# Main products of two MLPs: moving columns and outputs in eights, 32 words apart

## The chip, the cores and the metric

One NeuronCore of a Trainium2 chip runs the kernel. The metric is the device time of one execution in microseconds (us); a number for a kernel is the median of several executions. The profile is of one execution, taken by the hardware profiler, in which time is counted from the first to the last instruction (the span).

## What is computed

12480 tokens of 128 numbers go through an attention over 32 inducing points, applied twice, then through two MLPs of width 2048. The first has a leaky activation with a slope per hidden unit, the second the square of a ReLU. All is float32.

```python
def mab(q, kv):                       # attention of q over kv
    a = softmax(scale * (q @ kv.T))
    return a @ kv
h = mab(inducing, x)                  # 32 x 128
x = mab(x, h)                         # 12480 x 128
h = x @ w_in                          # first MLP, 128 -> 2048 -> 128
x = (np.maximum(h, 0.0) + alpha * np.minimum(h, 0.0)) @ w_out
h = np.maximum(x @ w2_in, 0.0)        # second MLP, 128 -> 2048 -> 128
out = h * h @ w2_out
```

## The kernel before

A first stage (to about 45 us) loads and transposes x, sums up the first attention and converts weights. Then a main loop runs over 25 tiles of tokens, 21 of 512 tokens, 3 of 448 and one of 384 (`WIDTHS`, line 19), and over 16 chunks of the hidden width in each. Tokens lie along the moving columns of TensorE's products, so a product is 512, 448 or 384 columns wide.

The order is written out by hand: a loop over steps s (lines 816 to 830) issues, for each s, `l1_a` (chunk s of the first MLP's first layer), `l2_a` and `l2_split` (the second MLP's first layer, 24 and 25 steps behind), `l2_b` and `l1_b` (the second layers, 28 and 3 steps behind), and whatever `plan` holds for that step (attention of the next four tiles, conversion of weights). The engines take their instructions in that order.

Products are made in float32r. To keep accuracy an operand is split into a high and a low part, and `three` (line 688) adds up high x high, low x high and high x low in one PSUM bank. So a step has ten products: one in `l1_a` (line 679; there the tile `a_s` holds the high and low parts in its partitions), three each in `l1_b`, `l2_a` and `l2_b` (lines 689 to 691). One more per tile, `end_y1` at line 707, adds the linear part of the leaky activation. Each product has its own 128x128 weights, so each comes with a weight load (PEld in the profile).

In a step ScalarE makes g1h (line 683), r (723) and g2h (732) and VectorE makes g1l (685) and sq (725); GpSimd makes g2l (734), except in the last 24 steps, when VectorE does. They read PSUM or SBUF contiguously and write the tiles that the next products stream.

In the memory layout of this program all weights of main products and all 512-wide moving tiles start at word 8 of their group of 32 words. Tiles narrower than 512 live in 512-wide buffers, and `columns` (line 118) gives them the place from word 40 of the buffer on, that is word 16 of a group of 32. A 512-wide tile fills its buffer.

Of the kernel before, what the change touches and what calls it, by code (L numbers as in the profile page):

```python
# [19 lines left out]
T = 512  # L20
# [10 lines left out]
def attention_then_two_mlps(ctx: ExitStack, tc, x, inducing, w_in, w_out, alpha, w2_in, w2_out, out):  # L31
# [3 lines left out]
    nc = tc.nc  # L35
# [3 lines left out]
    P = 128  # L39
# [29 lines left out]
    def free_bank():  # L69
        turn[0] += 1  # L70
        return ms_bank() if turn[0] % 2 or main_loop else y2_bank()
# [3 lines left out]
    def keep_tile(name, shape, dt=F32):  # L75
        return keep.tile(shape, dt, name=name, tag=name)
# [39 lines left out]
    xT = keep_tile("xT", [P, N])  # L116

    def columns(v, w):
        return v if w == T else v[:, 40 : 40 + w]

    w1s = keep_tile("w1s", [P, DFF], F32R)
    wo_hi = keep_tile("wo_hi", [P, NCH, P], F32R)
# [8 lines left out]
    v_s = keep_tile("v_s", [P, P], F32R)  # L131
# [163 lines left out]
    def scores(g):  # L295
        b = ms_bank()
        for i, (t0, n, _, _) in enumerate(groups1[g]):
            nc.tensor.matmul(
                b[i * M : (i + 1) * M, :n], indT, xT[:, t0 : t0 + n], start=True, stop=True,
                tile_position=(0, i * M),  # L300
            )
        return b[:, :n]
# [64 lines left out]
    b = free_bank()  # L367
# [4 lines left out]
    for g in range(last):  # L372
        if g:
            run(convs[g - 1][:2])
        b = scores(g)
# [18 lines left out]
        if g == 2:  # L394
            b = y2_bank()
# [6 lines left out]
    b = scores(last)  # L402
# [6 lines left out]
    b = y2_bank()  # L409
# [9 lines left out]
    b = ms_bank()  # L419
# [25 lines left out]
    b = y1_bank()  # L445
# [15 lines left out]
    def new_a_s(t):  # L461
        a_s[t] = columns(att.tile([P, T], F32R, name="a_s", tag="a_s", bufs=5), wide[t])
        return a_s[t]
# [211 lines left out]
    def l1_a(i, other_bank):  # L675
        t, c = divmod(i, NCH)
        b = h2_bank() if other_bank else h1_bank()
        a, w = a_s[t], wide[t]
        nc.tensor.matmul(b[:, :w], w1s[: a.shape[0], c * P : (c + 1) * P], a, start=True, stop=True)  # L679

        tag = "g2" if i < EARLY and i % 2 else "g1"
        hi = columns(wk.tile([P, T], F32R, name="g1h", tag=tag + "h", bufs=4), w)
        nc.scalar.activation(hi, b[:, :w], AF.Relu)  # L683
        lo = columns(wk.tile([P, T], F32R, name="g1l", tag=tag + "l", bufs=4), w)
        nc.vector.scalar_tensor_tensor(lo, b[:, :w], 0.0, f32(hi), op0=ALU.max, op1=ALU.subtract)  # L685
        g1[i] = hi, lo

    def three(b, w_hi, w_lo, hi, lo, start, stop):
        nc.tensor.matmul(b, w_hi, hi, start=start, stop=False)  # L689
        nc.tensor.matmul(b, w_lo, hi, start=False, stop=False)  # L690
        nc.tensor.matmul(b, w_hi, lo, start=False, stop=stop)  # L691

    def l1_b(i):
        t, c = divmod(i, NCH)
        if c == 0:
            y1_cur[t] = y1_bank() if t != 1 else y2_bank()
        b = y1_cur[t][:, : wide[t]]
        hi, lo = g1.pop(i)
        three(b, wo_hi[:, c, :], wo_lo[:, c, :], hi, lo, c == 0, False)
        if c == NCH - 1 and t:  # L700
            end_y1(t)

    def end_y1(t):
        w = wide[t]
        b = y1_cur.pop(t)[:, :w]
        a = a_s.pop(t)
        nc.tensor.matmul(b, v_s[: a.shape[0]], a, start=False, stop=True)  # L707
        hi = columns(wk.tile([P, T], F32R, name="y1h", tag="y1h", bufs=2), w)
        nc.scalar.copy(hi, b)
        lo = columns(wk.tile([P, T], F32R, name="y1l", tag="y1l", bufs=2), w)  # L710
        nc.vector.tensor_tensor(lo, b, f32(hi), op=ALU.subtract)
        y1_split[t] = hi, lo

    def l2_a(i):
        t, c = divmod(i, NCH)
        w = wide[t]
        b = h2_bank()[:, :w]
        cols = slice(c * P, (c + 1) * P)
        three(b, *(w2[tag][:, cols] for tag in W2["w2_in"]), *y1_split[t], True, True)
        if c == NCH - 1:  # L720
            del y1_split[t]
        r = wk.tile([P, T], F32, name="r", tag="r", bufs=2)[:, :w]
        nc.scalar.activation(r, b, AF.Relu)  # L723
        sq = wk.tile([P, T], F32, name="sq", tag="sq", bufs=3)[:, :w]
        nc.vector.tensor_tensor(sq, b, r, op=ALU.mult)  # L725
        rr[i] = sq
# [10 lines left out]
    def l2_b(i):  # L737
        t, c = divmod(i, NCH)
        if c == 0:
            y2_cur[t] = y2_bank()  # L740
        w = wide[t]
        b = y2_cur[t][:, :w]
        hi, lo = g2.pop(i)
        cols = slice(c * P, (c + 1) * P)
        three(b, *(w2[tag][:, cols] for tag in W2["w2_out"]), hi, lo, c == 0, c == NCH - 1)
        if c == NCH - 1:

            o = wk.tile([P, T], F32, name="o", tag="o", bufs=2)[:, :w]
            del y2_cur[t]
            if t == NT - 1:  # L750
                return last_rows(b, o)
            nc.vector.transpose(o, b)
            dst = out[first_token[t] : first_token[t + 1], :].rearrange("(b i) (a j) -> a i b j", i=M, j=M)
            for a in range(P // M):
                nc.sync.dma_start(
                    out=dst[a], in_=o[a * M : (a + 1) * M, :].rearrange("i (b j) -> i b j", j=M)
                )
# [41 lines left out]
    at(13, convs[7][LO])  # L799
    at(16, split_v)  # L800
    at(20, end_y1, 0)
    for tiles in groups[1:]:
        for k, v in enumerate(second_attention(tiles)):
# [12 lines left out]
    for s in range(total + LAG2 + LAG2B + 4):  # L816
        if s < total:
            l1_a(s, s < LAG2 and s % 2)
        if 0 <= s - LAG2 < total:
            l2_a(s - LAG2)  # L820
        if 0 <= s - LAG2 - 1 < total:
            l2_split(s - LAG2 - 1)

        ends = [(l1_b, i) for i in l1_b_at.get(s, [])]
        if 0 <= s - LAG2 - LAG2B < total:
            ends.insert(0 if ends and ends[0][1] % NCH == 0 else len(ends), (l2_b, s - LAG2 - LAG2B))
        for f, i in ends:
            f(i)
        for f in plan.pop(s, []):
            f()  # L830
# [30 lines left out]
```

## Time and profile before

| | |
|---|---|
| median of 3 executions | 961.35 us (961.16 to 964.46) |
| span of the profiled execution | 959.4 us (the time of that execution as a whole isn't listed apart) |
| TensorE busy | 949.3 us, 99% of the span |
| weight loads (they overlap products) | 787.6 us, 82% |
| ScalarE, VectorE, GpSimd busy | 727.4, 649.9, 536.9 us |
| granted TensorE clock, mean | 0.999 of full speed |

Busy time of TensorE is made of lengths of pipelined instructions, of which several are under way at once; how fast products follow each other is read from their starts in the timeline. In a row of section 5 of the page, the numbers behind the bar are the busy time in us, the mean length of one in ns, and the idle time of the engine before them.

### The profile page before, as it was taken

What the parts mean: (1) busy time and instruction counts of PE and PEld (TensorE: products, weight loads), DVE (VectorE), ACT (ScalarE), POOL (GpSimd) and SP (SyncE); (2) the same over time, 40 slices, a digit from 0 to 9 for tenths busy, and PEclk for the clock granted to TensorE, in tenths of its full rate; (3) what the DMA queues carried; (4) which work ended last, traced back from release to release, by engine and by line L of the source; (5) the groups of instructions that cost most, each with busy time, mean ns of one, the idle gap of its engine ahead of it and who ended that gap; (6) DMA issues with size and microseconds to landing.
All of it is one profiled execution on the core that took longest, in us unless ns stands there. A gap on an engine that the chain in (4) does not pass through costs nothing.

```text
span 959.4 us, 13675 instructions
## 1 busy us (share of the span) xinstructions
PE 949.3 (99%) x4560; PEld 787.6 (82%) x4560; DVE 649.9 (68%) x1013; ACT 727.4 (76%) x1333; POOL 536.9 (56%) x435
## 2 busy tenths in 40 slices
PE   9989999999999999999999999999999999999998
PEld 7667778888878888878888878888888888899997
DVE  5788767666667766667666667766666766666677
ACT  5779777777777777777777777777777777777776
POOL 2548755655555655555665555565555665555530
PEclk9999999999999999999999999999999999999999
DMA  9542000020000020000020000020000020000000
GB/s 343 163 111 82 1 12 12 9 47 12 1 12 12 3 52 12 1 12 12 1 55 12 1 12 1 12 55 1 12 12 1 12 48 1 12 12 4 8 11 19
DMA packets 64551, 29.00 MB, mean 30 GB/s; under 512 B 52208, under 2 KB 57440, under 8 KB 64480
## 3 DMA queue, kind: packets, MB, share of 16 engines
q1 hardware_dynamic: 64000, 27.52, 11.5%
q8 instruction: 36, 0.59, 0.3%
q10 hardware_dynamic: 480, 0.61, 0.2%
q14 instruction: 35, 0.29, 0.1%
HBM read 14.80 MB, written 6.39 MB: 22 GB/s over the span
## 4 chain that ended last, share of the span: by engine, by line
PE 89%; ACT 2%; DVE 1%; issue 1%; POOL 0%; POOLq 0%; DVEq 0%
PE y L691 17%; PE y L690 17%; PE y L689 17%; PE h L689 9%; PE h L690 9%; PE h L691 9%; PE h L679 8%; PE y L707 1%; PE ms L524 1%; ACT g1h L683 0%; ACT r L723 0%; DVE mag L199 0%; ACT g2h L732 0%; ACT raw L195 0%; DVE mag L205 0%
## 5 line engine op out<-in xcount | busy, mean ns | idle before, releaser
L734 POOL TENSOR_TENSOR g2l<-sq,g2h 128x512 fp32r<-128x512 f32 (+1 forms) x376 | 480.0, 1278 | 342.6 <-ACT g2h L732 331.6
L685 DVE SCALAR_TENSOR_TENSOR g1l<-h,g1h 128x512 fp32r<-128x512 f32 (+2 forms) x400 | 270.0, 677 | 230.3 <-ACT g1h L683 225.1
L683 ACT ACTIVATE g1h<-h 128x512 fp32r<-128x512 f32 (+2 forms) x400 | 234.2, 588 | 141.9 <-PE h L679 140.7
L725 DVE TENSOR_TENSOR sq<-h,r 128x512 f32<-128x512 f32 (+2 forms) x400 | 271.1, 678 | 53.9 <-ACT r L723 16.9
L723 ACT ACTIVATE r<-h 128x512 f32<-128x512 f32 (+2 forms) x400 | 235.8, 589 | 61.2 <-PE h L691 16.8
L732 ACT CAST g2h<-sq 128x512 fp32r<-128x512 f32 (+2 forms) x400 | 240.8, 602 | 2.6 <-DVE sq L725 2.6
L679 PE MATMUL h<-a_s,w1s 128*128 128x512 f32 (+3 forms) x400 | 155.0, 389 | 2.8 <-DMA a_s<-a_lo 1.4
L689 PE MATMUL h<-y1h,w2i_hi 128*128 128x512 f32 (+2 forms) x400 | 154.3, 386 | 0.3
L690 PE MATMUL y<-g2h,w2o_lo 128*128 128x512 f32 (+2 forms) x400 | 153.8, 385 | 0.0
L691 PE MATMUL h<-y1l,w2i_hi 128*128 128x512 f32 (+2 forms) x400 | 153.8, 384 | 0.0
L690 PE MATMUL h<-y1h,w2i_lo 128*128 128x512 f32 (+2 forms) x400 | 153.7, 384 | 0.0
L691 PE MATMUL y<-g2l,w2o_hi 128*128 128x512 f32 (+2 forms) x400 | 153.7, 384 | 0.0
L689 PE MATMUL y<-g2h,w2o_hi 128*128 128x512 f32 (+2 forms) x400 | 153.7, 384 | 0.0
L691 PE MATMUL y<-g1l,wo_hi 128*128 128x512 f32 (+2 forms) x400 | 153.7, 384 | 0.0
L690 PE MATMUL y<-g1h,wo_lo 128*128 128x512 f32 (+2 forms) x400 | 153.7, 384 | 0.0
L689 PE MATMUL y<-g1h,wo_hi 128*128 128x512 f32 (+2 forms) x400 | 153.7, 384 | 0.0
L679 PEld LDWEIGHTS h<-a_s,w1s 128*128 128x128 f32 (+1 forms) x400 | 75.0, 188 | 25.3 <-DVE sq L725 4.1
L689 PEld LDWEIGHTS h<-y1h,w2i_hi 128*128 128x128 f32 x400 | 75.1, 188 | 16.1 <-DVE sq L725 1.8
L690 PEld LDWEIGHTS y<-g1h,wo_lo 128*128 128x128 f32 x400 | 75.1, 188 | 14.8
L689 PEld LDWEIGHTS y<-g1h,wo_hi 128*128 128x128 f32 x400 | 75.1, 188 | 14.3
L691 PEld LDWEIGHTS y<-g2l,w2o_hi 128*128 128x128 f32 x400 | 75.1, 188 | 14.2 <-DVE g2l L734 0.3
L691 PEld LDWEIGHTS y<-g1l,wo_hi 128*128 128x128 f32 x400 | 75.1, 188 | 13.9
(156 smaller groups left out, 664.5 us busy)
## 6 DMA issues: line engine op xcount, KB each, us to landing
out_dram<-o SPq DMA_DIRECT2D x84, 64.0 KB, 2.0
xg<-in_x_dram SPq DMA_DIRECT2D x8, 512.0 KB, 9.1
raw<-in_moe_w_in_dram SPq DMA_DIRECT2D x8, 512.0 KB, 5.7
raw<-in_moe_w_out_dram SPq DMA_DIRECT2D x8, 512.0 KB, 4.6
a_s<-a_hi SPq DMA_DIRECT2D x40, 64.0 KB, 2.0
a_s<-a_lo SPq DMA_DIRECT2D x40, 64.0 KB, 2.0
x_last<-in_x_dram SPq DMA_DIRECT2D x2, 512.0 KB, 9.9
out_dram<-o SPq DMA_DIRECT2D x12, 56.0 KB, 1.9
```

The lines of the kernel that those rows point to most:

```text
L524: nc.tensor.matmul(b[i * M : (i + 1) * M, :w], hT[:, :M], xT[:, first_token[t + 1] - w : first_token[t + 1]], start=True, stop=True, tile_ ...
L679: nc.tensor.matmul(b[:, :w], w1s[: a.shape[0], c * P : (c + 1) * P], a, start=True, stop=True)
L683: nc.scalar.activation(hi, b[:, :w], AF.Relu)
L685: nc.vector.scalar_tensor_tensor(lo, b[:, :w], 0.0, f32(hi), op0=ALU.max, op1=ALU.subtract)
L689: nc.tensor.matmul(b, w_hi, hi, start=start, stop=False)
L690: nc.tensor.matmul(b, w_lo, hi, start=False, stop=False)
L691: nc.tensor.matmul(b, w_hi, lo, start=False, stop=stop)
L707: nc.tensor.matmul(b, v_s[: a.shape[0]], a, start=False, stop=True)
L723: nc.scalar.activation(r, b, AF.Relu)
L725: nc.vector.tensor_tensor(sq, b, r, op=ALU.mult)
L732: nc.scalar.copy(hi, sq)
L734: (nc.vector if i >= total - LAG2 else nc.gpsimd).tensor_tensor(lo, sq, f32(hi), op=ALU.subtract)
```

## The change

Each main product's moving operand and output are given as a pattern of four dimensions instead of two: for a tile of w columns, column 32a + 8b + c (a from 0 to w/32 - 1, b from 0 to 3, c from 0 to 7) is taken in the order b, a, c. The moving operand and the output go through the same pattern, so every result stands where it stood. Weights, tiles, buffers and the order of instructions are as before. `columns` now gives narrow tiles the buffer from word 0 on.

```diff
     def columns(v, w):
-        return v if w == T else v[:, 40 : 40 + w]
+        return v[:, :w]
+
+    def eights(v):
+        return v.rearrange("p (a b c) -> p b a c", b=4, c=8)
...
-        nc.tensor.matmul(b[:, :w], w1s[: a.shape[0], c * P : (c + 1) * P], a, start=True, stop=True)
+        nc.tensor.matmul(
+            eights(b[:, :w]), w1s[: a.shape[0], c * P : (c + 1) * P], eights(a), start=True, stop=True
+        )
...
     def three(b, w_hi, w_lo, hi, lo, start, stop):
+        b, hi, lo = eights(b), eights(hi), eights(lo)
         nc.tensor.matmul(b, w_hi, hi, start=start, stop=False)
         nc.tensor.matmul(b, w_lo, hi, start=False, stop=False)
         nc.tensor.matmul(b, w_hi, lo, start=False, stop=stop)
...
-        nc.tensor.matmul(b, v_s[: a.shape[0]], a, start=False, stop=True)
+        nc.tensor.matmul(eights(b), v_s[: a.shape[0]], eights(a), start=False, stop=True)
```

## Rows read from the trace of the kernel before

**Rows 1.** The page: busy us, share and instructions; granted clock in 40 slices.

```profile
PE 949.3 (99%) x4560; PEld 787.6 (82%) x4560; DVE 649.9 (68%) x1013; ACT 727.4 (76%) x1333; POOL 536.9 (56%) x435
...
PEclk9999999999999999999999999999999999999999
```

**Rows 2.** The chain by engine; TensorE's longest wait (us in total, times, longest).

```profile
PE 89%; ACT 2%; DVE 1%; issue 1%; POOL 0%; POOLq 0%; DVEq 0%
...
PE h L679 <- DMA a_s<-a_lo: 1.4, 1, 1.4
```

**Rows 3.** Timeline of TensorE, 512-wide tiles (start us, length us, instruction).

```profile
105.12 0.39 PE L679 MATMUL h<-a_s,w1s 128*128 128x512 f32 x1
105.35 0.39 PE L689 MATMUL h<-y1h,w2i_hi 128*128 128x512 f32 x1
...
127.79 0.39 PE L679 MATMUL h<-a_s,w1s 128*128 128x512 f32 x1
```

**Rows 4.** Timeline, products (PE) and weight loads (PEld) side by side.

```profile
500.25 0.39 PE L689 MATMUL y<-g2h,w2o_hi 128*128 128x512 f32 x1
500.26 0.19 PEld L690 LDWEIGHTS y<-g2h,w2o_lo 128*128 128x128 f32 x1
...
500.48 0.39 PE L690 MATMUL y<-g2h,w2o_lo 128*128 128x512 f32 x1
500.48 0.19 PEld L691 LDWEIGHTS y<-g2l,w2o_hi 128*128 128x128 f32 x1
```

**Rows 5.** Timeline of TensorE, narrow tiles: ten products of 448; 60 of 384 and 448.

```profile
867.00 0.36 PE L679 MATMUL h<-a_s,w1s 128*128 128x448 f32 x1
...
869.00 0.36 PE L679 MATMUL h<-a_s,w1s 128*128 128x448 f32 x1
...
904.80 0.34 PE L679 MATMUL h<-a_s,w1s 128*128 128x384 f32 x1
...
916.16 0.34 PE L679 MATMUL h<-a_s,w1s 128*128 128x384 f32 x1
```

**Rows 6.** Timeline of TensorE where tiles of 448 and 512 alternate.

```profile
828.65 0.37 PE L679 MATMUL h<-a_s,w1s 128*128 128x448 f32 x1
828.86 0.39 PE L689 MATMUL h<-y1h,w2i_hi 128*128 128x512 f32 x1
829.09 0.40 PE L690 MATMUL h<-y1h,w2i_lo 128*128 128x512 f32 x1
829.33 0.40 PE L691 MATMUL h<-y1l,w2i_hi 128*128 128x512 f32 x1
829.56 0.36 PE L689 MATMUL y<-g1h,wo_hi 128*128 128x448 f32 x1
...
830.86 0.37 PE L679 MATMUL h<-a_s,w1s 128*128 128x448 f32 x1
```

**Rows 7.** Float32 transposes: timeline, then groups by form (busy us, mean ns).

```profile
29.84 1.58 PE L286 MATMUL h<-ident,xg 128*128 128x128 f32 x13
31.25 0.64 PE L339 MATMUL y<-ident,e 128*128 128x128 f32 x4
...
L339 PE MATMUL y<-ident,e 128*128 128x128 f32 x24 | 4.0, 288 | 0.1
...
L286 PE MATMUL h<-ident,x_last 128*128 128x128 f32 x16 | 2.0, 276 | 0.0
```

**Rows 8.** The page's costliest groups (busy us, mean ns of one, idle before).

```profile
L734 POOL TENSOR_TENSOR g2l<-sq,g2h 128x512 fp32r<-128x512 f32 (+1 forms) x376 | 480.0, 1278 | 342.6 <-ACT g2h L732 331.6
...
L683 ACT ACTIVATE g1h<-h 128x512 fp32r<-128x512 f32 (+2 forms) x400 | 234.2, 588 | 141.9 <-PE h L679 140.7
...
L723 ACT ACTIVATE r<-h 128x512 f32<-128x512 f32 (+2 forms) x400 | 235.8, 589 | 61.2 <-PE h L691 16.8
L732 ACT CAST g2h<-sq 128x512 fp32r<-128x512 f32 (+2 forms) x400 | 240.8, 602 | 2.6 <-DVE sq L725 2.6
L679 PE MATMUL h<-a_s,w1s 128*128 128x512 f32 (+3 forms) x400 | 155.0, 389 | 2.8 <-DMA a_s<-a_lo 1.4
```

## The prediction

> **What bounds the kernel now.** I read the page's busy shares first, then the chain and the waits, then the timeline of TensorE by its starts. TensorE is busy for 99% of the span with the granted clock at its upper level, 2.4 GHz, in nearly all slices [rows 1]. It is 89% of the chain, and its longest wait in all is 1.4 us, once [rows 2]. So what counts is the distance from one matmul's start to the next one's. The busy times of section 5 mislead here: they are lengths of pipelined instructions that overlap. A 512-wide main product is given 0.39 us, but the next one starts after 0.23 [rows 3].
>
> Between the starts at 105.12 and 127.79 us lie exactly 100 main products, all 512 wide [rows 3]: 22.67 us / 100 = 226.7 ns each. At 2.4 GHz 512 columns take 213.3 ns, so each one pays **13.3 ns** on top of its columns. The rest does not grow with width: ten 448-wide ones take 2.00 us, 200.0 ns each against 186.7 for the columns, 13.3 again; and 60 products from 904.80 to 916.16 us (24 of 384, 36 of 448) take 11.36 us against 10.56 for their columns, 13.3 each once more [rows 5]. It is a price per matmul, not per column.
>
> Two readings tell what the price is made of. First, the float32 transposes also change their weights at every matmul and pay much less: 13 of them fill 1.58 us, of which the last one's own length is 0.276, so starts are (1.58 - 0.276) / 12 = 108.7 ns apart. If a float32 column takes two column times (its cadence fits that and no smaller whole number), 128 of them take 106.7 ns and 2.0 ns are left [rows 7]. There the moving operand is read at half the rate. So about 11.3 ns of the 13.3 come only when the stream runs at full rate. Second, the price depends on where the words lie: where 448-wide tiles (which start 40 words into their buffer) alternate with 512-wide ones (which start at word 0), ten products, four and six of them, take 830.86 - 828.65 = 2.21 us against 4 x 186.7 + 6 x 213.3 = 2.027, so **18.3 ns** each, and the same form of product varies by 10 ns within the group [rows 6]. Each kind by itself pays 13.3. What runs under each product is the weight load for the next one: it starts within 0.01 us of the product's start and lasts 0.19 us [rows 4]. My reading is that the load's reads and the moving stream's reads get in each other's way, by place.
>
> **The change part by part.** No instruction is added, removed or moved between engines; the order on each engine is the old one. Four things differ.
>
> (1) The moving operand of all main products: 10 groups of 400 (one of them in [rows 8]) and one per tile at the end of the first MLP, 25, so 4025. Instead of words 0, 1, 2, ... the stream takes eight words at each of 16 places 32 words apart, then the next eight at each, four rounds. Within one round of 128 columns (53 ns) it stays at one place modulo 32 words, while the load below it goes through 128 consecutive words, that is four times through all four places. What does that do to the 11.3 ns? No row has this order, so I bound it. Lowest: the load and the stream no longer meet, 2.0 ns are left, 11.3 x 4025 = 45.5 us gained. Highest: the lucky spacing of [rows 3] is lost and every product pays what the mixed tiles pay, 18.3 ns: 5.0 x 4025 = 20.1 us lost. I take a value near the lower end: if all 16 eights of a load now delay the stream (the stream passes through all four places again and again, and after a delay follows the load into the next one), and in the new order only those can that lie at the stream's present place, one in four, then 11.3 / 4 = 2.8 ns remain: 2.0 + 2.8 = 4.8 ns, a gain of 8.5 ns each, **8.5 x 4025 = 34.2 us**. The "all" is an assumption; it is what rival 3 disputes.
>
> (2) The output is written in the same eights into PSUM. The price of a jump: the nearest row is the transpose that reads its moving operand four words apart, a new place for each column. Four of them fill 0.64 us, (0.64 - 0.288) / 3 = 117 ns apart against 108.7 for contiguous ones, 8.6 ns for 128 jumps [rows 7], 0.07 ns a jump. A 512-wide product now has 64 jumps: 4.3 ns by that price, 17 us in all. That is the upper bound on the reading side; the lower is nothing, since the transposes jump at 128 places and half rate and an eight gives far more time between jumps. I take nothing for reads. For jumps of the output there is no row at all; I take nothing too and leave the rest to rival 4.
>
> (3) Narrow tiles start at word 0 of their buffer, so that all products lie at one place. If the alternation in [rows 6] costs 5.0 ns a product more than the others, about 290 products from 790 to 855 us lose 1.4 us now; in the new order both kinds take the same rounds. It is within (1), and I add nothing.
>
> (4) ScalarE, VectorE and GpSimd read and write the same tiles contiguously as before. For one step of ten products, 2.27 us now, ScalarE has 588 + 589 + 602 = 1.78 us, GpSimd 1.28 us [rows 8]; at the forecast's 2.18 us per step, or at 2.15 with the whole price gone, neither becomes the bound. If GpSimd's or ScalarE's cover went, a step could not go under 1.78 us anyway, far off. Some waits for semaphores disappear near the tail and two appear on TensorE for its own results; they cost nothing where the queue is in order.
>
> **Sum.** 34.2 us off the span of 959.4 gives 925.2. The median of the runs, 961.35, is 1.95 us over this span, so the forecast is **927 us**.
>
> One rule of the skill speaks against the mechanism. The Trainium skill, TensorE: Matmul & The Clock Gate, Part 2, step by step, says that TensorE has two independent SBUF read ports and that loading the next weights doesn't steal read bandwidth from the running matmul. By that rule the new order of reads changes nothing, and the sum would be 961. The trace doesn't settle it, but [rows 6] show a price that depends on the words' places, which two free ports don't explain.
>
> **The rivals.**
> Rival 2, no change: the 13.3 ns are the cost of changing full-rate weights, whatever is read. For it: the same 13.3 at three widths [rows 3, 5]. Against it: 18.3 in the mixture [rows 6]. Time: 961.
>
> Rival 3, slower by lost spacing: already now only a quarter of the load's words meet the stream, since both go through the four places alternately; the new order meets just as many, and the regular spacing of [rows 3], which is the best that the old order settles into, is gone. Then all products pay the 18.3 of the mixture: 961 + 20.1 - 1.4 = **980 us**. It decides from the point where what meets in the new order delays the stream by more than the 11.3 ns of now. That 13.3 is a favourable case and not the rule is what [rows 6] show.
>
> Rival 4, slower by jumps: jumps of the moving operand or of the output cost more than the meetings save. At 0.07 ns a jump and no gain it is 961 + 17 = 978; at one column time a jump (0.42 ns at 2.4 GHz) 64 x 0.42 = 26.7 ns a product, 107 us, 1068. It overcomes the forecast's gain from 8.5 / 64 = 0.13 ns a jump.
> This is also what a page would make of it: the Trainium skill, Advanced Engine Details and Errata, PSUM Cachelines, says that any non-contiguous pattern slows matmuls significantly, and in the next line that every two consecutive elements should be contiguous for best throughput. By the first sentence rival 4 holds, by the second eights are long enough; no run here shows either.
>
> **How the numbers follow.** Forecast, meetings mostly gone: 0.50, with its own range from 914 (all 45.5 + 1.4 us) to 944 (half of the 11.3 ns stays: 22.7 us gained, less some jumps). Rival 2: 0.12. Rival 3: 0.22, 966 to 985. Rival 4: 0.16, mostly above 985. The range that leaves out no more than 2 in 10 goes from 914 to 985: outside lie most of rival 4 and a little below. A measurement of this kernel can tell about 0.5% from no change: faster by more 0.50, within 0.12, slower by more 0.38.
>
> **What would show it.** In the changed kernel's timeline, 100 products in the stretch where all tiles are 512 wide should take about 21.8 us instead of 22.67 (218 ns from start to start); 21.5 would be the whole price, 22.67 rival 2, 23.2 rival 3, over 24 rival 4. The stretch from 828 us on, wherever it then lies, should show the same price per product as the pure stretches, since places no longer differ. Lengths of ScalarE's and VectorE's instructions should be unchanged, and TensorE's waits still near 1 us each; if instead waits for g1h, g2l or r grow, another engine has become the bound, and the step (4) is wrong. A price that grows with width (512 against 448 and 384) would show a cost per jump; one that doesn't is a matter of the weight load.

## The result: two times, and two rhythms

The changed kernel takes 936 to 939 us in some executions and 969 to 972 us in others, and nothing between: 969.87, 972.13, 936.15 and 938.75 us in the first comparison (median 954.31; the kernel before 961.25), and 938.01, 968.67, 935.85, 969.36, 969.85 and 970.05 us in the second (median 969.02). The ratio to the kernel before is 0.975 (95% interval 0.972 to 0.978), counting the shorter executions alone; the longer ones, six of ten, are 0.9% slower than before, and the mean of all ten, 956.9 us, is about 0.5% below it. The forecast was 927 us, with 914 to 985 as range.

Profiles exist of both kinds: the first comparison left one of 969.87 us (span 968.1), the second one of 938.01 us (span 936.2). The page of the longer one first, with the rows that answer to [rows 1] and [rows 8]: busy us, share and instructions of each engine; the granted clock in 40 slices; then a group of GpSimd and one of ScalarE with busy us and mean ns of one.

```profile
PE 958.4 (99%) x4560; PEld 791.3 (82%) x4560; DVE 649.8 (67%) x1013; ACT 727.9 (75%) x1333; POOL 533.8 (55%) x435
...
PEclk9899999999999999999999999999999999999999
...
L740 POOL TENSOR_TENSOR g2l<-sq,g2h 128x512 fp32r<-128x512 f32 (+1 forms) x376 | 476.9, 1269 | 352.0 <-ACT g2h L738 315.5
...
L688 ACT ACTIVATE g1h<-h 128x512 fp32r<-128x512 f32 (+2 forms) x400 | 234.0, 588 | 147.3 <-PE h L682 147.0
```

TensorE is still busy for 99%, the clock is at its upper level, and the other engines' instructions last as long as before. What differs between the two kinds is the distance of the products' starts. The timeline of TensorE in the longer execution (start us, length us, instruction; the first row and the one 100 products later, then two products in a row, then the one 100 products after 140.02):

```profile
107.45 0.38 PE L682 MATMUL h<-a_s,w1s 128*128 128x512 f32 x1
...
129.45 0.38 PE L682 MATMUL h<-a_s,w1s 128*128 128x512 f32 x1
...
140.02 0.39 PE L682 MATMUL h<-a_s,w1s 128*128 128x512 f32 x1
140.25 0.39 PE L695 MATMUL h<-y1h,w2i_hi 128*128 128x512 f32 x1
...
163.08 0.39 PE L682 MATMUL h<-a_s,w1s 128*128 128x512 f32 x1
```

100 products take 129.45 - 107.45 = 22.00 us, **220.0 ns** each (a price of 6.7 on top of the 213.3 for the columns, where before paid 13.3 [rows 3]). After the interruption by attention's scores at 131 us the same products take 23.06 us per 100, **230.6 ns** each, a price of 17.3. Call the first the good rhythm and the second the bad one. By the trace's starts, which are finer than the two decimals of the rows, the good one alternates 219 and 221 ns, and the bad one repeats five distances of 227, 229, 230, 230 and 237. The weight loads themselves last 187 to 190 ns in either, as before (0.19 us in [rows 4]); what differs is what a product pays besides. The bad one outlives four more interruptions and ends where tiles of 448 and 512 begin to alternate. There, with the good rhythm, the group that answers to [rows 6] reads:

```profile
819.22 0.35 PE L682 MATMUL h<-a_s,w1s 128*128 128x448 f32 x1
819.41 0.38 PE L695 MATMUL h<-y1h,w2i_hi 128*128 128x512 f32 x1
...
821.32 0.35 PE L682 MATMUL h<-a_s,w1s 128*128 128x448 f32 x1
```

Ten products take 2.10 us against 2.027 for their columns: some 7 ns each instead of 18.3. In the short execution the good rhythm holds from about 105 us to the mixture and through it (ahead of 103 us it too runs in the bad one); its page's row of the engines, and 100 products behind the same interruption:

```profile
PE 925.9 (99%) x4560; PEld 786.6 (84%) x4560; DVE 649.6 (69%) x1013; ACT 727.9 (78%) x1333; POOL 534.5 (57%) x435
```

```profile
106.83 0.38 PE L682 MATMUL h<-a_s,w1s 128*128 128x512 f32 x1
...
139.05 0.38 PE L682 MATMUL h<-a_s,w1s 128*128 128x512 f32 x1
...
161.05 0.38 PE L682 MATMUL h<-a_s,w1s 128*128 128x512 f32 x1
...
860.42 0.35 PE L682 MATMUL h<-a_s,w1s 128*128 128x448 f32 x1
```

161.05 - 139.05 = 22.00 us again. The first and the last of these rows are the 218th and the 3,649th main product. Those two in the kernel before are the first row of [rows 3] and this one:

```profile
883.00 0.36 PE L679 MATMUL h<-a_s,w1s 128*128 128x448 f32 x1
```

So the 23.2 us between the spans (959.4 and 936.2) are found in one place. Between these two products the kernel before takes 883.00 - 105.12 = 777.9 us, the short execution 860.42 - 106.83 = 753.6 and the long one, where the later of them starts at 892.25, 892.25 - 107.45 = 784.8. That is 24.3 us gained or 6.9 lost; the rest (1.7 to 2.3 us more ahead of them, 0.6 less behind) lies outside the long run of products.

Behind it the gain ends. From the first 384-wide products on (870 us in the short execution, 902 in the long one) the good rhythm is lost in both. These two rows of the short execution are 60 products apart, 24 of 384 and 36 of 448:

```profile
882.58 0.34 PE L695 MATMUL y<-g1h,wo_hi 128*128 128x384 f32 x1
...
893.90 0.34 PE L695 MATMUL y<-g1h,wo_hi 128*128 128x384 f32 x1
```

They take 11.32 us, a price of 12.7 ns each, where before paid 13.3 [rows 5]. Why 384 columns break the rhythm stays open.

### The profile page after: what moved, and what is told of

The parts are those of the page before. It is cut to its first block, busy times and chain, and to the rows that moved or that the text cites. A ratio compares the mean times of both kernels' runs of the same rounds, so it can differ in the third digit from the quotient of the medians.

```text
span 968.1 us, 13652 instructions
## 1 busy us (share of the span) xinstructions
PE 958.4 (99%) x4560; PEld 791.3 (82%) x4560; DVE 649.8 (67%) x1013; ACT 727.9 (75%) x1333; POOL 533.8 (55%) x435
## 4 chain that ended last, share of the span: by engine, by line
PE 92%; DVE 0%; ACT 0%; issue 0%; DVEq 0%; ACTq 0%
PE y L697 18%; PE y L695 18%; PE y L696 18%; PE h L695 9%; PE h L696 9%; PE h L697 9%; PE h L682 9%; PE y L713 1%; PE ms L527 1%; DVE g1l L690 0%; DVE sq L731 0%; ACT r L729 0%; PE h L775 0%; DVE o L771 0%; DVE r L777 0%
## 5 line engine op out<-in xcount | busy, mean ns | idle before, releaser
L740 POOL TENSOR_TENSOR g2l<-sq,g2h 128x512 fp32r<-128x512 f32 (+1 forms) x376 | 476.9, 1269 | 352.0 <-ACT g2h L738 315.5
```

The costliest lines, as they stand in the source:

```text
L740: (nc.vector if i >= total - LAG2 else nc.gpsimd).tensor_tensor(lo, sq, f32(hi), op=ALU.subtract)
```

## Experiments

The theories on trial: **T1**, the price is paid where the next weights' load and the moving stream meet, so it goes by the order in which columns are read, by the place of the weights against the moving tiles, and by when products start. Against it: **T2**, the 30 us between the two kinds are clock or transfers; **T3**, the order in which results are put back is what counts; **T4**, the price belongs to the change of weights as such; **T5**, the eights have their two prices by themselves, whatever the places, and something that lasts in an execution picks one.

### The changed kernel again

No edit.

> The changed kernel unaltered. Two theories of its time. (T1) Its main products run in one of two settled rhythms, which its profile already showed one after the other: 220.0 ns from start to start at 512 wide (6.7 ns above 213.3) and 230.7 ns (17.3 ns above). Which one holds is settled at the interruptions (start, attention). Then an execution that keeps the first from about 107 us on takes 961.4 - 4025 x 6.7 ns = 934 to 939 us and one that falls into the second at 133 us takes 970; times lie near these two values and between them only if a change of rhythm comes at another place; a profile of a short execution shows 219 and 221 ns alternating to the end. (T2) The rhythm of the products is the same in all executions and the difference lies elsewhere (DMA or clock): then a profile of a short execution shows 230.7 ns too, and the 30 us come out of waits of over 260 ns or a granted clock under 1.

The times fall into the two groups, and the profile of 938.01 us alternates 219 and 221 ns (in one stretch a steady 220) to the end of the full tiles, as shown above. T2 falls: the distances themselves differ, with the clock at its upper level in both.

### Seventeen orders in one execution

```diff
+    def rounds(b, c):
+        return lambda v: v.rearrange("p (a b c) -> p b a c", b=b, c=c)
+    SURVEY = {
+        4: (plain, plain), 5: (eight, eight), 6: 2 * (rounds(8, 4),),
...
     def eights(v):
-        return v.rearrange("p (a b c) -> p b a c", b=4, c=8)
+        return orders()[0](v)
+
+    def outs(v):
+        return orders()[1](v)
```

> The changed kernel, with another order of the moving columns in every block of 16 steps (some 36 us each, 160 products and more), so that one execution shows the price above 213.3 ns of each. In order of the blocks from step 64 on, written as columns in a piece x pieces in a round, with places a piece length apart: in a row; eights x 4 (the changed kernel's); fours x 8; sixteens x 2; eights x 8; fours x 16; twos x 8; fours x 4; eights x 4 for the moving columns alone; eights x 4 for the results alone; thirty-twos x 2; eights x 2; sixteens x 4; twos x 16; twos x 32; eights x 4 again; in a row again. In the blocks with the order on one side alone results land in other columns, so the output is not the reference's; nothing is left out. (T1, the order in which columns are read decides, by place against the next weights' load) the block with moving columns alone has the price of eights, 6.7 or 17.3 ns, the one with results alone the 13.3 ns of a row; orders whose pieces jump a multiple of 32 words between neighbours differ from those that jump 16 words. (T3, the order in which results are put back decides) the other way round: results alone 6.7 or 17.3, moving alone 13.3. (T4, the price belongs to the change of weights and is 13.3 ns with any order; the two rhythms come from when the products start) blocks of all orders show 6.7, 13.3 or 17.3 ns with no relation to the order, and eights need not come out at 6.7 or 17.3.

In `rounds(b, c)` the second number is the columns in a piece; the product of the two is the distance in words from one piece to the next. The view is the table of stretches (ten of the seventeen): us from and to, length, TensorE's busy time with the instructions under way in it, granted clock, then DMA share and GB/s. A stretch counts one or two products that had begun before it, so distances here are taken from starts inside it.

```profile
206.00:238.00 32.00, 32.00 (x140) 1.00 0.06 9
242.00:275.00 33.00, 33.00 (x135) 1.00 0.05 8
290.00:320.00 30.00, 30.00 (x126) 1.00 0.06 10
...
362.00:396.00 34.00, 34.00 (x124) 1.00 0.05 9
...
480.00:505.00 25.00, 25.00 (x112) 1.00 0.07 11
518.00:545.00 27.00, 27.00 (x119) 1.00 0.23 49
555.00:580.00 25.00, 25.00 (x112) 1.00 0.07 11
...
705.00:770.00 65.00, 65.00 (x139) 1.00 0.03 5
...
862.00:885.00 23.00, 23.00 (x107) 1.00 0.08 12
895.00:920.00 25.00, 25.00 (x112) 1.00 0.12 29
```

| stretch from | piece, distance (words) | start to start, ns | price, ns |
|---|---|---|---|
| 170, 895 | in a row | 226.7, 226.7 | 13.3 |
| 206 | 8, 32 (the change) | 230.7 | 17.3 |
| 862 | 8, 32 (the change) | 220.0 | 6.7 |
| 518 | 8, 32, moving columns alone | 230.6 | 17.3 |
| 555 | 8, 32, results alone | 226.7 | 13.3 |
| 242 | 4, 32 | 246.7 | 33.3 |
| 290 | 16, 32 | 240.0 | 26.7 |
| 705 | 2, 32 | 473.3 | 260 |
| 330, 362 | 8 and 4, 64 | 233.3, 278.1 | 20.0, 64.8 |
| 664, 590 | 16 and 32, 64 | 239.5, 236.7 | 26.2, 23.3 |
| 785 | 2, 64 | 486.7 | 273 |
| 628, 480, 410 | 8, 4 and 2, 16 | 232.3, 226.8, 431.1 | 19.0, 13.4, 218 |

On the two orders that decide T3, 100 products each in TensorE's timeline, first moving columns alone in eights, then results alone:

```profile
519.93 0.40 PE L718 MATMUL y<-g2h,w2o_lo 128*128 128x512 f32 x1
...
542.99 0.40 PE L718 MATMUL y<-g2h,w2o_lo 128*128 128x512 f32 x1
...
557.10 0.39 PE L719 MATMUL y<-g2l,w2o_hi 128*128 128x512 f32 x1
...
579.77 0.39 PE L719 MATMUL y<-g2l,w2o_hi 128*128 128x512 f32 x1
```

These are 23.06 us (230.6 ns each) and 22.67 (226.7). T3 falls: results put back in eights with the columns read in a row keep 226.7 ns, and moving columns in eights with results in a row pay what both together pay in that rhythm. T4 falls: with prices from 6.7 to 273 ns it follows the order. What also falls is any simple rule of distance: as seen here, fours and sixteens 32 words apart are worse than a row, and only eights 32 words apart, in one of their two rhythms, are better. Every other order was seen once, so a second, better rhythm of one of them is not excluded. Twos pay 218 to 273 ns, of the size of a second reading of the columns (213.3). The Trainium skill says of SBUF that subsequent accesses to one 16-byte line are at full performance and that it takes at least two such hits to hide the memory's latency (Advanced Engine Details and Errata, SBUF Cachelines). Twos, half such a line, touch each line just twice before they leave it and cost about double; fours, a whole line, clear that mark and still pay 13.4 to 64.8. So the rule by itself does not give these prices.

### Narrow tiles at word 0, alone

```diff
-        return v if w == T else v[:, 40 : 40 + w]
+        return v[:, :w]
```

> The kernel before with only the third part of the change: tiles narrower than 512 begin at word 0 of their buffer, not at word 40; columns in a row. (T1) 512-wide products keep 13.3 ns each; what changes is the mixed stretch at about 790 to 855 us, where 18.3 ns were paid with the 448 tiles at word 40: if their place was the cause it falls to 13.3 ns, some 290 products x 5 ns = 1.5 us, 959.9 in all. (Rival: mixing of widths as such breaks the rhythm) the stretch keeps 18 ns, and the time is 961.4. Neither gives the 22 to 25 us between the kernel before and the shorter executions of the changed one.

The time was 964.05 us, and the mixture stays dear. Ten products of the mixture, and 20 products of 448 alone further on, in TensorE's timeline:

```profile
814.80 0.37 PE L679 MATMUL h<-a_s,w1s 128*128 128x448 f32 x1
...
816.99 0.37 PE L679 MATMUL h<-a_s,w1s 128*128 128x448 f32 x1
...
858.17 0.36 PE L679 MATMUL h<-a_s,w1s 128*128 128x448 f32 x1
...
862.23 0.36 PE L679 MATMUL h<-a_s,w1s 128*128 128x448 f32 x1
```

The mixture takes 2.19 us for ten, 16 ns each above the columns, not 13.3; and the 448 tiles by themselves, which paid 13.3 at word 40 [rows 5], take about 203 ns each, a price of 16. From the 218th to the 3,649th main product it takes 777.8 us, as before. What the mixture gains the pure 448 stretch loses. The spans differ by 2.9 us in this one execution (962.3 against 959.4), and all of it lies ahead of the 218th product (1.8) and behind the 3,649th (1.1); in the latter part, with tiles of 384 among those of 448, products pay 16 to 19 ns on average instead of 13.3.

### Weights moved in SBUF, columns in a row

```diff
+    keep_tile("gap_a", [P, 16])
     w1s = keep_tile("w1s", [P, DFF], F32R)
...
+    keep_tile("gap_b", [P, 16])
     al = keep_tile("al", [P, NCH])
```

> The kernel before with every weight tile moved on by 16 words in SBUF; moving columns in a row, at their old places, and all instructions the same. (T1, weights' load and moving stream meet by the place of their words) the price of the 512-wide products changes from 13.3 ns, or the products don't settle into 226.7 ns from start to start: anywhere between 6.7 and 18 ns, thus 934 to 980 us; that the price stays would need that 16 words make the same meetings. (T4, the price belongs to the change of weights whatever their place) 226.7 ns and 961.4 us.

One thing of this text is wrong: the second gap lies ahead of the moving tiles too, so these moved by 32 words and the weights by 16, and what changed is that weights stand 16 words back against the columns. 100 products of full width:

```profile
139.51 0.39 PE L681 MATMUL h<-a_s,w1s 128*128 128x512 f32 x1
...
162.40 0.39 PE L681 MATMUL h<-a_s,w1s 128*128 128x512 f32 x1
...
328.04 0.40 PE L693 MATMUL h<-y1l,w2i_hi 128*128 128x512 f32 x1
...
351.37 0.40 PE L693 MATMUL h<-y1l,w2i_hi 128*128 128x512 f32 x1
```

The first two rows are 22.89 us apart, 228.9 ns each: a price of 15.6 instead of 13.3, and 975.36 us. No instruction is different, only addresses. It speaks for T1 and against T4. The last two rows show a second rhythm, 23.33 us per 100 or 233.3 ns each, a price of 20.0. It holds in four stretches of 32 to 38 us, one tile of tokens long at most; each begins at the one product of `end_y1` at the end of a tile, whose weights moved by 32 words and not by 16, and three of them end at the next such product. So two settled rhythms are nothing peculiar to eights: columns in a row have them too once the weights stand elsewhere.

### Extra products between

```diff
+        if i > 40 and i % 4 == 0:
+            k = 16 + 8 * (i // 4 * 5 % 14)
+            nc.tensor.matmul(b[:, :k], w1s[:, :P], w1s[:, :k], start=True, stop=True)
```

> The changed kernel with one extra product of 16 to 120 columns (in steps of 8, in turn) ahead of the first layer's product in every fourth step from step 44 on, into a bank that the next product starts afresh: nothing else changes. Each extra product moves the start of all that follows. (T1, which of the two settled rhythms holds is a matter of when the products start) the rhythm changes again and again between 220.0 and 230.7 ns in the 90 or so stretches of 40 products, each settled within some ten products, and which one follows goes by the length of the extra product and the rhythm before; some lengths may lead to 220.0 ns from either. (T5, the rhythm is set by something that lasts, such as where transfers or the buffers of an execution lie) it stays 220.0 or 230.7 ns from one interruption by attention to the next, whatever is put between. The extra products cost some 90 x 40 ns = 4 us beside that; time 940 to 975 us by T1, at either end by T5.

955.53 us, with all the extra products. The timeline around one of 48 columns:

```profile
256.36 0.40 PE L699 MATMUL y<-g1h,wo_lo 128*128 128x512 f32 x1
256.60 0.39 PE L700 MATMUL y<-g1l,wo_hi 128*128 128x512 f32 x1
...
257.51 0.18 PE L684 MATMUL h<-w1s 128*128 128x48 f32 x1
257.54 0.47 PE L685 MATMUL h<-a_s,w1s 128*128 128x512 f32 x1
257.85 0.38 PE L698 MATMUL h<-y1h,w2i_hi 128*128 128x512 f32 x1
...
259.83 0.38 PE L685 MATMUL h<-a_s,w1s 128*128 128x512 f32 x1
```

Ahead of it a distance of 0.24 in the pattern of the bad rhythm; behind it nine products in 259.83 - 257.85 = 1.98 us, 220.0 ns. From 120 to 785 us there are 73 stretches between extra products. 66 end in the good rhythm and seven in the bad one; all seven bad ones were ended by the next extra product (of 48 columns four times, of 32 twice, of 104 once). Of 65 good ones six turned bad, after lengths of 120 (three times), 104 (twice) and 64 (once, with attention's scores in between). The same length does not always lead to the same rhythm (120 columns led three times from good to bad and twice from good to good). So the rhythm is set by when products start, and T5's lasting cause falls: of the products behind, nothing but the start times changed. Which start leads to which rhythm was not worked out.

### Places of the tiles

```diff
+    PLACES = (0, 8, 16, 24, 4, 12, 20, 28, 0)
-    def columns(v, w):
-        return v[:, :w]
+    def columns(v, w, t):
+        k = PLACES[t // 3]
+        return v[:, k : k + w]
...
-        a_s[t] = columns(att.tile([P, T], F32R, name="a_s", tag="a_s", bufs=5), wide[t])
+        a_s[t] = columns(att.tile([P, T + 32], F32R, name="a_s", tag="a_s", bufs=5), wide[t], t)
```

with the extra products above, and the other moving tiles in the same way.

> The changed kernel with the same extra products, and with the moving tiles begun at word 0, 8, 16, 24, 4, 12, 20, 28 and again 0 of buffers 32 words longer, for three tiles (48 steps) each; weights stay where they are. The results' square has two buffers instead of three and the output one instead of two, which should cost nothing. (T1, price by the place of weights against moving columns, modulo 32 words, and by start) the prices of the settled rhythms differ from place to place, and some place may have one rhythm only, at 6.7 ns or less. (T5, place of no weight: two rhythms of the eights' order by themselves) 6.7 and 17.3 ns at every place. The kernel before with weights moved by 16 words paid 15.4 ns instead of 13.3, which speaks for T1. Time 930 to 985 us.

986.45 us, and inconclusive on the single places: with buffers 544 words long, neighbours stand 32 words apart modulo 64, and from the first tiles on, still at word 0, no rhythm settled; the products between two extra ones pay 12 to 22 ns on average. That it might matter whether all tiles stand alike modulo 64 words was not expected; the next runs move the weights alone.

### Weights moved, columns in eights

Four runs with the extra products and one edit; the gaps always add to 128 words, so moving tiles stay where they were modulo 128 and only the weights move, here by 8 words:

```diff
+    keep_tile("gap_a", [P, 8])
     w1s = keep_tile("w1s", [P, DFF], F32R)
...
+    keep_tile("gap_b", [P, 120])
     al = keep_tile("al", [P, NCH])
```

> The changed kernel with the extra products of 16 to 120 columns in every fourth step, and all weights moved on by 8 words in SBUF against the moving tiles (which stay where they were modulo 128 words). (T1, the price goes by the place of weights against moving columns) other settled rhythms than 220.0 and 230.7 ns, lower or higher: 5 to 20 ns a product, 930 to 990 us with the extra products. (T5, only the eights' order counts, whatever the places) the same two, mostly 220.0 ns, and 955 us as with the weights in place.

> As the run before it, with the weights moved on by 16 words. (T1) rhythms other than 220.0 and 230.7 ns; with columns in a row such a move raised the price from 13.3 to 15.4 ns. (T5) 220.0 ns mostly, 955 us.

> As the two runs before it, with the weights moved on by 32 words. The pieces that are read one after another stand 32 words apart. (T1 with places that count modulo 32 words) the same rhythms as with the weights in place, 220.0 and 230.7 ns, 955 us. (T1 with places that count modulo 64 words or more) other rhythms; the run with moving tiles in buffers 544 words apart, where neighbours stand 32 words apart modulo 64, lost the settled rhythms from its first tile on and paid some 20 ns, which speaks for this. (T5) as the first.

> The changed kernel with the extra products of 16 to 120 columns in every fourth step, and all weights moved on by 24 words. With 8, 16 and 32 words the settled rhythms were 226.7, 228.9 and about 229 ns instead of 220.0, and the times 981 to 984 us, which bore out that the place of the weights sets the price. (T1) again another settled price, between 5 and 18 ns; if it is under 6.7 ns, the weights' place is a lever of its own: under 950 us with the extra products, otherwise 955 to 990. (Rival: only a distance of 0 gives less than the 13.3 ns of columns in a row) 13 to 18 ns, 975 to 990 us.

980.55, 980.76, 984.31 and 993.18 us (8, 16, 32 and 24 words). Ten products each in the timelines, for 8, 16 and 24 words:

```profile
162.38 0.39 PE L687 MATMUL h<-a_s,w1s 128*128 128x512 f32 x1
...
164.65 0.39 PE L687 MATMUL h<-a_s,w1s 128*128 128x512 f32 x1
```

```profile
160.84 0.39 PE L687 MATMUL h<-a_s,w1s 128*128 128x512 f32 x1
...
163.12 0.40 PE L687 MATMUL h<-a_s,w1s 128*128 128x512 f32 x1
```

```profile
164.71 0.39 PE L687 MATMUL h<-a_s,w1s 128*128 128x512 f32 x1
...
167.03 0.40 PE L687 MATMUL h<-a_s,w1s 128*128 128x512 f32 x1
```

2.27, 2.28 and 2.32 us: settled prices of 13.3 (a pattern of 225, 226 and 229 ns), 15.6 and 20.0 ns (226, 240 and 234). With 8 words that holds for 52 of 70 stretches between extra products, the others end at 19 to 23 ns; with 16 and 24 words all end alike. With 32 words the products pay 15 to 21 ns, from stretch to stretch, and hardly settle. T5 falls, and with it the thought that places count only modulo 32 words. The good rhythm's 6.7 ns were seen only with the weights where the changed kernel happens to have them, in step with the moving tiles. Nor is it the load that gets longer: with 24 words most loads last 187 to 192 ns, in the good rhythm 187 to 188. The Trainium skill (TensorE: Matmul & The Clock Gate, Part 2, step by step) says that the weights' load has a read port of its own and takes no read bandwidth from the running matmul. These runs, in which only the weights' place differs and the spacing goes from 220.0 to 226.7, 228.9 and 233.3 ns, speak against that for float32r products at full rate, though they don't show what the two share.

### A few extra products to leave the bad rhythm

```diff
+    RELOCK = {36, 50, 82, 114, 146, 178, 210, 242, 274, 306, 338}
...
+        if i in RELOCK:
+            nc.tensor.matmul(b[:, :48], w1s[:, :P], w1s[:, :48], start=True, stop=True)
```

> The changed kernel with an extra product of 48 columns, into a bank that the next product starts afresh, ahead of the first layer's product in steps 36, 50 and then every 32nd up to 338: eleven in all. In the run with extra products in every fourth step, every one of 48 columns led into 220.0 ns from start to start, four times from 230.7 ns and otherwise from 220.0, at a cost of 27 ns and some 86 ns ahead of the next product. (T1, the rhythm is a matter of when products start) all executions run at 220.0 ns from about 107 us on, with at most 32 steps in the other rhythm after an interruption: 936 to 938 us as the shorter executions of the changed kernel have it, and 11 x 0.11 = 1.2 us: 937 to 942 us in every execution, and none near 970. (T5, the extra products only happened to fall into executions of the one kind) two groups of times as for the changed kernel, near 938 and near 971.

944.41, 945.90, 938.92, 945.76, 940.89 and 946.10 us; 0.981 of the kernel before (0.978 to 0.983). None is near 970, but four lie above the 942 that T1 was given. The profile (span 942.6) shows why:

```profile
100.85 0.18 PE L684 MATMUL h<-w1s 128*128 128x48 f32 x1
100.88 0.47 PE L685 MATMUL h<-a_s,w1s 128*128 128x512 f32 x1
...
103.99 0.49 PE L685 MATMUL h<-a_s,w1s 128*128 128x512 f32 x1 [0.65 <-DVE g1l L693]
```

The first extra product leads to the good rhythm for some eight products; then a wait for g1l sets the start times anew, and the bad one follows. The second, in step 50, comes ten products behind attention's scores and ends in the bad one too. The third, at 210 us, leads to 220.0 ns, and every later one keeps it. So 48 columns do not always help: out of a bad rhythm that had long been settled they did in six of six cases (four in the run before), ten products behind an interruption they did not.

With five, behind the wait and the unsettled products (`RELOCK = {40, 52, 60, 116, 180}`):

> The changed kernel with five extra products of 48 columns, ahead of the first layer's product in steps 40, 52, 60, 116 and 180. In the run with eleven of them the one in step 36 lay ahead of the pause at 103 us and the one in step 50 within ten products of an interruption, and the rhythm of 230.7 ns held from 107 to 210 us; the one in step 82 ended it, and every later stretch kept 220.0 ns. (T1) the five, put behind the pause and some 40 products behind the interruption at 132 us, end the longer rhythm by about 160 us at the latest; each costs 0.1 to 0.2 us: 936 to 940 us in all executions. (T5) some executions at 968 to 971 us.

936.59, 936.33 and 936.77 us, but also 952.54, 949.53 and 949.79: median 943.15, ratio 0.981 (0.976 to 0.987). The profile is one of 936.59 us and shows only good rhythm. What the longer three do wasn't profiled. By size, 13 us are some 1,250 products at 10.6 ns more, two of the stretches of 64 steps between attention's scores; which interruption starts it stays open. Both versions beat the kernel before in every execution and the changed kernel on its median; neither holds the good rhythm always.

## Why the prediction came out as it did

**What bounds the kernel** held: TensorE 99% busy before and after, and all of the difference lies in the starts of main products.

**Term (1), the order of the moving columns.** The mechanism was right in kind: the price depends on reading order and places, and eights can take it down. The size was off twice. The sum had 8.5 ns off each product, leaving 4.8; the good rhythm leaves 6.7, so 6.7 are gained (226.7 - 220.0). And from the 218th to the 3,649th product 24.3 us came in the short executions, where 8.5 x 3431 would be 29.2. The failed step is the one in four: that the price shrinks with the share of the load's pieces that can lie at the stream's place, and that there is one price. By that rule fours at the same distance would have paid some 3.4 ns (2.0 + 11.3 / 8) and sixteens some 7.7 (2.0 + 11.3 / 2); they pay 33.3 and 26.7. And the eights themselves have a second settled rhythm at 17.3 ns. The 2.0 ns of the transposes, taken as what is left without meetings, showed up in no run either: the least is 6.7.

**Term (2), jumps.** Nothing, as taken. Results alone in eights keep 226.7 ns, and in the good rhythm products of 448 and 512 pay the same 6.7 ns, so none per column or jump. But the 0.07 ns a jump that bounded the term, and rival 4's 978 with it, came from a misread row. In the transposes the operand named second is the one that is loaded as weights, as in the main products, and the form of a smaller one in the kernel before shows it (weights 128x48, moving columns 128x128):

```profile
L339 PE MATMUL y<-ident,e 128*48 128x128 f32 x1 | 0.4, 401 | 0.0
```

So what is read four words apart is the weights, e, while the moving `ident` lies in a row: the 8.6 ns go with a scattered weight load, and no row of before had a jump of the moving operand. For shorter pieces a price exists: 218 to 273 ns with twos; which side of the product pays it wasn't told apart there.

**Term (3), narrow tiles at word 0.** The reading that their place was the cause of the 18.3 ns was wrong: alone it leaves 16 in the mixture and costs 3 ns a product in the pure 448 stretch, in sum nothing up to the 3,649th product and about 1 us behind it. In the changed kernel the mixture is cheap where the eights' good rhythm holds across 448 and 512 columns; eights with narrow tiles at their old place were not run, so the share of each is not shown.

**Term (4), the other engines.** Unchanged lengths (1269 and 588 ns, against 1278 and 588 [rows 8]), and no new bound at a step of 2.20 us.

**Rivals.** Rival 2 is refuted by the survey. Rival 4's mechanism is refuted for eights. Rival 3 (spacing lost, 18.3 ns each, 980 us) is what the longer executions come near to: 17.3 ns and 970 us. Both were in one kernel, so forecast and rival 3 were not alternatives between which the chip decides once; each execution chose anew. A hint that one form can have several prices stood in the rows: it varied by 10 ns within the mixture [rows 6]. The prediction used that variation for places only; that start times choose was shown by the extra products alone.

**The number.** 927 is 9 to 12 us under the shorter executions and 42 to 45 under the longer ones; the range held both. That it held the longer ones is partly luck: its upper part was there for rival 3's mixed-tile price, and no rival had two prices in one kernel.

## What to carry to other kernels

Where TensorE is always busy, divide the time between two starts far apart by the count of products and compare it with the columns: what is left per product is a quantity of its own, here 13.3 of 226.7 ns, 5.9%. It can depend on where weights and moving tiles lie in SBUF and on the order of reading, so try moving one array by a few words before rewriting anything. Unlike places of the moving buffers went with unsettled and dearer products in the one run that had them. If single executions of one program fall into two times with the clock unchanged, look for two spacings in the timeline, and test it with a short extra product that shifts the starts.

## What the runs showed that was not expected

In most of these runs 512-wide products settle into repeating patterns within some ten products after a disturbance and can keep them for hundreds of microseconds: in eights two, of 220.0 and 230.7 ns, in a row one of 226.7, but two of 228.9 and 233.3 once the weights stood 16 words back. Where neighbouring moving buffers, or weights and moving tiles, stood 32 words off their usual distance they hardly settled. The settled prices are regular: prices of 6.7, 13.3, 20.0, 26.7 and 33.3 ns turn up for quite different orders, all multiples of 6.67 ns, which is 16 column times at 2.4 GHz; others (15.6, 17.3, 23.3) are means over patterns of several products. Weights moved by 8 words, with nothing else changed, cost 6.7 ns a product or more against the good rhythm. What exactly meets in SBUF is not settled by these runs: they show that reading order, the weights' place and the start times set the price, not by which conflict.
